# Sums of key features by ones-products for three blocks, r tiles 0 to 5 inside the M products, and loads and stores behind the transposed rows

## The chip, the cores and the metric

The kernel runs on 1 core of one Trainium2 chip. The metric is the device time of one execution in microseconds (us). The record also gives, for all runs but the first ones of the kernel before, the mean clock that was granted to TensorE, as a share of full speed. A kernel's *profile* shows one execution instruction by instruction; its length is called the *span*, and is some 1.7 us less than the device time of the same execution. No run here is recorded as slow. Kernels that were sent together ran on the same chip, and the kernel before ran in between them in the same rounds.

## The reference, cut to what matters

The result is the output of one transformer block (linear attention, then a gated MLP) and the gradients of all its inputs. Only the forward attention matters for the change:

```python
# S = 2048 rows, D = 640, 32 heads of 20
qkv = layernorm(x) @ wqkv
pq, pk = phi(q), phi(k)              # phi(t) = (t > 0 ? t + 1 : exp(t)) + 1e-6
kv  = einsum("bhsd,bhse->bhde", pk, v)
z   = einsum("bhsd->bhd", pk)        # the sums of the key features
num = einsum("bhqd,bhde->bhqe", pq, kv)
den = einsum("bhqd,bhd->bhq", pq, z)[..., None] + 1e-6
o   = num / den
h   = x + merge_heads(o) @ wo
# then h2 = h + mlp(layernorm(h)), and the gradients by jax.vjp
```

The kernel divides the features of a row by that row's `den` before they meet `kv`; the product `r = pq / den` is what is called r below. There are 16 row tiles of 128 rows, and 5 blocks of 128 feature columns.

## The kernel before

Its first 135 us go in this order: the rows are normalised and transposed, multiplied by wqkv to give key features (`pk_all`), which are in turn multiplied with the rows (the *M products*, one of five blocks at a time). Then come the small products that fold M, wqkv and wo into one matrix Wp, and then the residual and the MLP. Into these the q tiles and the r tiles are woven. Helpers and order, with cuts:

```python
def phi(acc, dst, then=None):          # a q tile: exp, relu on ScalarE, the rest on VectorE later
    ...
    A.activation(two(mq[:]), acc[:, :, 0:HD], AF.Exp)
    A.activation(two(rq[:]), acc[:, :, 0:HD], AF.Relu)
    def rest():
        V.tensor_scalar(out=mq[:], in0=mq[:], ..., op0=ALU.min, op1=ALU.add)      # L276
        V.tensor_tensor(out=dst, in0=mq[:], in1=rq[:], op=ALU.add)                # L277
    held.append(rest)

def z_late(ms, acc):                   # key sums: one-column products with ones
    for t in range(ST):
        for i, m in enumerate(ms):
            T.matmul(acc[:, i:i + 1], lhsT=pk_all[:, t, m * P:(m + 1) * P], rhs=ones[:, 0:1], ...)
    A.copy(out=Z[:, ms[0]:ms[-1] + 1], in_=acc[:, 0:len(ms)])
    for m in ms:
        z_diag(m)

def z_row(ms, acc):                    # the sums as a row on all partitions: Zb
    ...
    A.copy(out=Zb[...], in_=acc[:, 0:len(ms) * P])                                # L324

def r_prod(t):                         # pq * Zb: GpSimd for t < 6, else VectorE
    ...
    (G if t < 6 else V).tensor_tensor(out=pr[t, j], in0=pqs[t][:, js], in1=Zb[:, js], op=ALU.mult)

def r_red(t):   ... V.reduce_sum(...)                                             # L343
def r_inv(t):   ... V.tensor_scalar(... add 1e-6); V.reciprocal(...)              # L346, L347
def r_scale(t): ... V.tensor_tensor(... pqs[t] * 1/den)                           # L350
def r_T(t):     dmaT(out=pqT[:, :, t * P:(t + 1) * P], in_=pqs[t])   # transposing DMA, SyncE queue

# the K loop: trickle holds the loads of wqkv's last part, w1, w3 and wo, in this order
for t in range(ST):
    k = p1_mm(t, D)
    ...
    if i == 1 and g > 0:
        group_out(g - 1)               # stores pk (and, for the first two groups, the rows)
    elif t >= 2 and trickle:
        trickle.pop(0)()

# the M products, blocks 1 to 4 (cut)
m_end(1)
z_late((3, 4), big())                  # blocks 0 to 2 get their sums as a 321st column of M
m_part(2, range(8))
z_row((0, 1), big())
q_tile(5)
m_part(2, range(8, ST))
m_end(2)
...
m_part(3, range(5))
z_row((2, 3, 4), big())
r_prod(0)
...                                    # three r tiles are finished in this stage, five more later
```

Of the kernel before, what the change touches and what calls it, by code (L numbers as in the profile page):

```python
# [9 lines left out]
P = 128  # L10
# [45 lines left out]
def kernel(  # L56
# [119 lines left out]
    def load_wq(a, b):  # L176
        dma(out=wqkv[:, :, a * HD:b * HD], in_=wq_v[:, :, a * HD:b * HD])
# [42 lines left out]
    def load_w13(c0, c1):  # L220
        def go1():
            dma(out=w1[:, c0:c1, 0:F], in_=rows(B_w1)[:, c0:c1, :])

        def go3():
            dma(out=w3[:, c0:c1, :], in_=rows(B_w3)[:, c0:c1, 0:F - FL])
        return [go1, go3]
# [101 lines left out]
    def r_prod(t):  # L328
        for j in range(2):
            js = slice(j * HD, (j + 1) * HD)  # L330
            if t < 6:
                pr[t, j] = (p1.tile([P, HD], F32, name="pr", bufs=2) if t % 2 else
                            pf.tile([P, HD], F32, name="pr", tag="h2", bufs=2))[:]
            else:
                pr[t, j] = ps.tile([P, 512], F32, name="prp", tag="at", bufs=2)[:, 0:HD]
            (G if t < 6 else V).tensor_tensor(out=pr[t, j], in0=pqs[t][:, js], in1=Zb[:, js], op=ALU.mult)

    def heads(ap):
        return ap.rearrange("p (h e) -> p h e", e=DH)
# [40 lines left out]
    def m_part(m, tiles):  # L380
        if m not in macc:
            macc[m] = [ps.tile([P, 512], F32, name="macc", tag=("m", "tr")[m % 2], bufs=2) for _ in range(2)]
        for t in tiles:
            for j, n in enumerate((HD, HD + (m < 3))):
                T.matmul(macc[m][j][:, 0:n], lhsT=pk_all[:, t, m * P:(m + 1) * P],  # L385
                         rhs=x_ext[:, t, j * HD:j * HD + n], start=(t == 0), stop=(t == ST - 1))

    def m_end(m):
        mb = mbs[:, m % 4, :]
        acc = macc.pop(m)  # L390
        for j in range(2):
            A.copy(out=mb[:, j * HD:(j + 1) * HD], in_=acc[j][:, 0:HD])
        if m < 3:
            A.copy(out=Z[:, m:m + 1], in_=acc[1][:, HD:HD + 1])
            z_diag(m)
        if m < DT - 1:
            dmaT(out=mT[:, :, m * P:(m + 1) * P], in_=mb)
# [13 lines left out]

    def load_w2T(a, b):
        dmaT(out=w2T[:, :, a:b], in_=B_w2[a:b, :])

    trickle = []

    zero_pads()
    load_w2T(0, 2 * P)
# [19 lines left out]
            ln1.part(x_sb, t + 1, 0)  # L438
            p1_norm(t)
    ln1.part(x_sb, 3, 1)  # L440
    trickle += [lambda: load_wq(4, 6)]
    for c0, c1 in ((0, 2), (2, 4), (4, 5)):
        trickle += load_w13(c0, c1)
    trickle += [lambda: dma(out=w1[:, :, F:FP], in_=rows(B_w3)[:, :, F - FL:F])]
    trickle += [lambda: dma(out=wo[:], in_=A_wo.rearrange("(c p) n -> p c n", p=P))]



    stat_of = {t: (t + 4,) for t in range(7)}
    stat_of.update({7: (11, 12), 8: (13,), 9: (14,), 10: (15,)})  # L450
# [7 lines left out]
    def group_out(g):  # L458
        sl = slice(g * TPC, (g + 1) * TPC)
        dma(out=pk_v[:, sl, :], in_=pk_all[:, sl, :])  # L460
        if g < 2:
            xn_out(g, dma)

    QT = (5, 7, 9, 11)
    for t in range(ST):
        g, i = divmod(t, TPC)
        k = p1_mm(t, D)
        if t < 3:
            p1_tr(t + 1, ((0, 2), (2, DT)))
        for n in stat_of.get(t, ()):  # L470
            ln1.run(x_sb, n, n + 1)
            if on_act(n):
                ln1.bias(n)
        for n in norm_of.get(t, ()):
            if not on_act(n):
                p1_norm(n)
        phi_rest(t < 4)
        phi(k, pk_all[:, t, :])
        for n in norm_of.get(t, ()):
            if on_act(n):  # L480
                p1_norm(n)
        if t in QT:
            q_tile(QT.index(t))
        if 2 <= t < 6:
            ghh_chunk(t - 2, ps.tile([P, 2, 512], F32, name="gp", tag="big", bufs=2)[:, 0])
            p1_tr(t + 2)
        if t >= 3:
            m_part(0, [t - 3])
        if t >= 11:
            V.memset(bd[:, t - 11, :], 0.0)  # L490
            make_mask(t - 11)
        if t >= 9:
            m_part(1, [2 * (t - 9), 2 * (t - 9) + 1])
        if i == 1 and g > 0:
            group_out(g - 1)
        elif t >= 2 and trickle:
            trickle.pop(0)()
    phi_rest()
    group_out(SC - 1)

    def big():
        return ps.tile([P, 2, 512], F32, name="bigx", tag="big", bufs=2)[:, 0]

    q_tile(4)
    m_part(0, (13, 14, 15))
# [1 line left out]
    phi_rest()  # L507
    m_part(1, (14, 15))
    m_end(1)
    z_late((3, 4), big())  # L510
    m_part(2, range(8))
    z_row((0, 1), big())
    q_tile(5)
    m_part(2, range(8, ST))
    m_end(2)
    load_w2T(4 * P, 8 * P)
    phi_rest()
    m_part(3, range(5))
    z_row((2, 3, 4), big())
    r_prod(0)  # L520
    q_tile(6)
    m_part(3, range(5, 11))
    phi_rest()
    r_red(0)
    r_inv(0)
    r_prod(1)
    q_tile(7)
    kvT_block(0, big())
    m_part(3, range(11, ST))
    phi_rest()  # L530
    r_scale(0)
    r_T(0)
    r_red(1)
    r_inv(1)
    r_prod(2)
    m_end(3)
    load_g2T(1)
    dmaG(out=m_v[:, 0:4, :], in_=mbs[:])
    m_part(4, range(5))
    q_tile(8)  # L540
    kvT_block(1, big())
    m_part(4, range(5, 11))
    phi_rest()
    r_scale(1)
    r_T(1)
    r_red(2)
    r_inv(2)
    r_prod(3)
    q_tile(9)
    m_part(4, range(11, ST))  # L550
    m_end(4)
    r_prod(4)
    phi_rest()
    r_scale(2)
    r_T(2)
    ps.release()
    load_x(0, 2)
    while trickle:
        trickle.pop(0)()


    ps = pool("pap", space=PSUM)
# [74 lines left out]
    def r4_out():  # L637
        dmaG(out=r_v[:, 0:4, :], in_=pq6[:, 0:4, :])

    def r4b_out():  # L640
        dmaG(out=r_v[:, 4, :], in_=pqs.pop(4))

    def r_load(t):
        pqs[t] = pf.tile([P, D], BF16, name="pql", bufs=4)[:]
# [131 lines left out]
    def run(*steps):  # L776
# [4 lines left out]
    pkx.append(p1.tile([P, DT + 6, D], BF16, name="pkx", tag="pk"))  # L781
    run((q_late, 10, f2_mT), (f2_kv, 2), (f2_kv, 3), (f2_kv, 4), (phi_rest,), (q_late, 11), (f2_wT, 0), (f2_wT, 1),
        (phi_rest,), (q_late, 12), (f2_wT, 2), (f2_wT, 3), (phi_rest,), (q_late, 13, lambda: f2_wT(4)),
        (r_red, 3), (r_inv, 3), (r_scale, 3), (r_prod, 5), (load_x, 2, 4), (r_T, 3), (q_late, 14), (r_red, 4),
        (r_inv, 4), (r_scale, 4), (r_T, 4), (load_x, 4, 8), (mlp_ghh, 4), (q_late, 15),
        (sig_table,), (f2_half, 0, 0), (f2_half, 1, 0), (f2_half, 0, 1), (f2_half, 1, 1), (f2_hn, 0), (mlp_ghh, 5),
        (f2_half, 2, 0), (f2_hn, 1), (f2_m_out,), (load_w2T, 8 * P, 10 * P), (f2_half, 2, 1),
        (f2_ht, 0), (mlp_ghh, 6), (f2_half, 3, 0), (f2_hn, 2), (f2_w_out,), (f2_ht, 1), (f2_half, 3, 1), (phi_rest, 2),
        (q_out, 10, 14), (f2_ht, 2), (f2_hn, 3), (mlp_ghh, 7), (f2_half, 4, 0), (f2_ht, 3),
        (f2_half, 4, 1), (r4_out,), (r_red, 5), (r_inv, 5), (r_scale, 5), (r_out, 5), (r4b_out,), (q_out, 8, 10))  # L790
    p1.release()
    pa = pool("pa", "right")

# [25 lines left out]
    def r_end(t):  # L819
        r_scale(t)  # L820
        r_out(t)

    r_steps = [{1: ((r_den, 6),), 2: ((r_end, 6), (r_load, 8)), 4: ((r_den, 7), (r_load, 9)), 5: ((r_end, 7),),
                6: ((xn_out, 2, dmaG),), 3: ((load_w2T, 10 * P, F),), 12: ((r_load, 10),), 13: ((xn_out, 3, dmaG),)},
               {0: ((r_den, 8),), 1: ((r_end, 8), (r_load, 11)), 2: ((r_den, 9),), 3: ((r_end, 9), (r_load, 12)),
                4: ((r_den, 10), (q_rest,)), 5: ((r_end, 10), (r_load, 13)), 6: ((r_den, 11),),
                7: ((r_end, 11), (r_load, 14)), 9: ((r_den, 12),), 10: ((r_end, 12), (r_load, 15))},
# [596 lines left out]
```

## Time and profile before

| | value |
|---|---|
| median of 3 timed runs | 839.07 us (838.42 to 840.68) |
| span of the profiled execution | 832.4 us (its device time was 834.09) |
| TensorE busy / idle in it | 819.1 / 13.3 us |
| its granted clock | 1.0 |

TensorE is busy nearly always, so the kernel can only be made faster by removing work from TensorE, by filling its idle stretches (*holes*), or by raising its clock. The prediction prints the lines. Note the difference of some 5 us in device time between the timed runs and the profiled one: it turns out to matter.

### The profile page before, as it was taken

To read this page: it belongs to the slowest core of one execution; us is meant where nothing else is said; L and a number is where in the kernel's file an instruction comes from. 1 tells how busy PE (TensorE), PEld (TensorE's weight loads), DVE (VectorE), ACT (ScalarE), POOL (GpSimd) and SP (SyncE) were. 2 spreads that over 40 slices of the span, in tenths; PEclk is the share of its full clock that TensorE was granted. 3 is DMA by queue.
4 is the path that set the end of the run, shared out by engine and by line. 5 is a ranking of instruction groups with operands and counts; after the bars stand their busy time and mean duration, and the time that the engine had idled before them with its cause. 6 is when DMAs were issued, how large, how long until landed. Compare 5 with 4: busy or idle time off the path is not lost.

```text
span 832.4 us, 14209 instructions
## 1 busy us (share of the span) xinstructions
PE 819.1 (98%) x5552; PEld 523.8 (63%) x5552; DVE 454.1 (55%) x964; ACT 319.5 (38%) x606; POOL 106.6 (13%) x156
## 2 busy tenths in 40 slices
PE   8899998999999999999999999999999999999998
PEld 6577644555555555777777777777777777555554
DVE  7847898999898656400047777772681445200000
ACT  6765777755555666111122221222211433211111
POOL 3214232122122010000001111110220000000000
PEclk9999999999999999999999999999999999999999
DMA  9986899786574465999968888346997688885771
GB/s 270 324 236 136 221 236 290 223 226 149 166 203 118 127 215 171 202 253 244 264 149 181 181 205 204 86 102 113 227 267 148 153 189 184 208 194 140 163 169 37
DMA packets 323315, 157.59 MB, mean 189 GB/s; under 512 B 235312, under 2 KB 318160, under 8 KB 323248
## 3 DMA queue, kind: packets, MB, share of 16 engines
q1 hardware_dynamic: 293696, 127.73, 64.0%
q10 hardware_dynamic: 24416, 11.23, 6.5%
q0 software_dynamic: 5136, 17.73, 6.1%
q8 instruction: 43, 0.70, 0.3%
q14 instruction: 24, 0.20, 0.1%
HBM read 48.15 MB, written 51.46 MB: 120 GB/s over the span
## 4 chain that ended last, share of the span: by engine, by line
PE 92%; DVE 3%; DMA 3%; ACT 1%; SPq 1%; issue 0%; DVEq 0%; ACTq 0%
PE job L1189 19%; PE mm L364 18%; PE ghn L991 14%; PE gxn L1348 8%; PE o L751 7%; PE gw L944 7%; PE big L255 3%; PE gwo L1076 3%; PE dkv L1292 3%; PE gr L1048 3%; PE macc L385 2%; PE at L573 2%; DMA pqT<-x_sb 1%; PE mm L255 1%; DMA g2T<-in_grad_out_dram 1%; DMA pqT<-pql 1%
## 5 line engine op out<-in xcount | busy, mean ns | idle before, releaser
L1189 PE MATMUL job<-gb,hnN 128*128 128x432 bf16 x640 | 117.0, 346 | 0.0
L991 PEld LDWEIGHTS <-ggb 128*128 128x128 bf16 x864 | 84.5, 98 | 32.8
L1189 PEld LDWEIGHTS <-hnN 128*128 128x128 bf16 x640 | 62.6, 98 | 54.1
L364 PE MATMUL mm<-pqT,w 128*128 128x512 bf16 x405 | 93.8, 379 | 1.3 <-ACT gate L693 1.2
L364 PEld LDWEIGHTS <-w 128*128 128x128 bf16 x540 | 52.8, 98 | 64.7 <-issue 1.8
L1193 ACT CAST obs<-job 128x432 bf16<-128x432 f32 (+1 forms) x60 | 29.2, 486 | 123.1 <-PE job L1189 120.7
L751 PE MATMUL o<-w,hhT 128*128 128x320 bf16 x448 | 67.5, 299 | 0.0
L364 PE MATMUL mm<-g2T,w2T 128*128 128x512 bf16 x260 | 64.6, 379 | 0.2 <-ACT gate L693 0.2
L991 PE MATMUL ghn<-w13a,ggb 128*128 128x320 bf16 x448 | 63.5, 299 | 0.0
L991 PE MATMUL ghn<-w13b,ggb 128*128 128x320 bf16 x416 | 61.4, 299 | 0.0
L751 PEld LDWEIGHTS <-hhT 128*128 128x128 bf16 x448 | 43.8, 98 | 23.6
L944 PE MATMUL gw<-g,hb 128*128 128x320 bf16 x416 | 57.0, 299 | 0.0
L374 ACT CAST ghh<-mm 128x512 bf16<-128x512 f32 x52 | 30.6, 589 | 53.7 <-PE mm L364 52.9
L944 PEld LDWEIGHTS <-hb 128*128 128x128 bf16 x416 | 40.6, 98 | 15.7
L1348 PE MATMUL gxn<-wqT,gT 128*128 128x320 bf16 x320 | 48.7, 299 | 0.0
L1056 POOL TENSOR_TENSOR sz<-Zb,g_h 128x640 f32<-128x640 bf16 x16 | 20.2, 1261 | 199.4 <-DVE g_h L1054 199.4
L691 ACT ACTIVATE sig<-mm 128x512 bf16<-128x512 f32 x56 | 33.6, 601 | 27.6 <-PE mm L364 24.6
L364 PEld LDWEIGHTS <-w2T 128*128 128x128 bf16 x280 | 27.2, 98 | 26.6 <-issue 1.7
L255 PE MATMUL big<-wqkv,pqT 128*128 128x320 bf16 x260 | 39.3, 299 | 4.0 <-DMA pqT<-x_sb 3.2
L1003 ACT ACTIVATE gs<-ghn 128x640 bf16<-128x640 f32 x16 | 11.3, 704 | 78.6 <-PE ghn L991 78.6
L255 PEld LDWEIGHTS <-pqT 128*128 128x128 bf16 x320 | 30.4, 98 | 17.0 <-DMA pqT<-x_sb 3.5
L1348 PEld LDWEIGHTS <-gT 128*128 128x128 bf16 x320 | 31.3, 98 | 12.2
(196 smaller groups left out, 1249.9 us busy)
## 6 DMA issues: line engine op xcount, KB each, us to landing
hh_d<-hhT SPq DMA_DIRECT2D x24, 256.0 KB, 2.8
gg_d<-gate SPq DMA_DIRECT2D x24, 256.0 KB, 3.1
gg_d<-ghh POOLq DMA_DIRECT2D x24, 256.0 KB, 3.3
ggb<-gg_d SPq DMA_DIRECT2D x6, 896.0 KB, 5.7
ggb<-gg_d SPq DMA_DIRECT2D x6, 832.0 KB, 7.0
out_dram<-obs ACTq DMA_DIRECT2D x40, 108.0 KB, 2.3
x_sb<-in_A_x_dram SPq DMA_DIRECT2D x6, 640.0 KB, 5.9
ggb<-gg_d SPq DMA_DIRECT2D x2, 1728.0 KB, 12.9
```

The lines of the kernel that those rows point to most:

```text
L255: T.matmul(acc, lhsT=pqT[:, c, t * P:(t + 1) * P], rhs=wqkv[:, c, n0:n0 + HD], start=(c == 0), stop=(c == DT - 1))
L364: T.matmul(acc[:], lhsT=w[:, c, fc * P:(fc + 1) * P], rhs=rhs[:, c, :], start=(c == 0), stop=(c == DT - 1))
L374: A.copy(out=ghh[n // 2][:, n % 2, :], in_=acc[:])
L691: A.activation(sig[:, i, :], gp[:], AF.Sigmoid)
L751: T.matmul(o2["ps"][:, 0:HD], lhsT=hhT[c][:, fc, i * P:(i + 1) * P], rhs=w2[:, fc, j * HD:(j + 1) * HD], start=(fc == 0), stop=(fc == FT - 1))
L944: T.matmul(acc[:, j, 0:HD], lhsT=hb[b][:, t, i * P:(i + 1) * P], rhs=g2[:, t, j * HD:(j + 1) * HD], start=(t == 0), stop=(t == ST - 1))
L991: T.matmul(acc[:, j, 0:HD], lhsT=ggb[t // 2][:, k, lo:lo + P], rhs=rhs[:, j * HD:(j + 1) * HD], start=(k == 0), stop=(k == NG - 1))
L1048: T.matmul(gr[t][:, j, 0:HD], lhsT=ghT[t][:, c, :], rhs=wT2[:, c, j * HD:(j + 1) * HD], start=(c == 0), stop=(c == DT - 1))
L1076: T.matmul(acc[m][:, j, 0:n], lhsT=r_sb[:, t, m * P:(m + 1) * P], rhs=g_hx[:, t, j * HD:j * HD + n], start=(t == 0), stop=(t == ST - 1))
L1189: T.matmul(acc[:, 0:n], lhsT=lhs[:, t, m * P:(m + 1) * P], rhs=rhs(t), start=(t == 0), stop=(t == ST - 1))
L1193: A.copy(out=ob, in_=acc[:, 0:n])
L1348: T.matmul(acc[:, j, 0:HD], lhsT=g, rhs=wqT[:, k, j * HD:(j + 1) * HD], start=(k == 0), stop=(k == 14))
```

## The change

Its intent is to fill the holes of the first 135 us. The last load of wqkv no longer stands ahead of the row transposes, and the stores meet them later; the key sums are complete one M block earlier, so that the r tiles can start earlier; six r tiles instead of three are then done inside the M products, and fewer are left for the crowded start of the MLP. The diff, cut to its core:

```diff
-            if t < 6:                                   # r_prod: which tiles GpSimd multiplies
+            if t < 8:
-            for j, n in enumerate((HD, HD + (m < 3))):  # block 2 loses its 321st column
+            for j, n in enumerate((HD, HD + (m < 2))):
-    trickle += [lambda: load_wq(4, 6)]
-    ... w1, w3, wo in the same list
+    trickle = {3: w13[0], 4: w13[1], 11: lambda: load_wq(4, 6), 12: w13[2], 14: w13[3], 15: load_wo}
+    outs = {6: ((group_out, 0),), 7: ((xn_out, 0, dma),), 10: ((group_out, 1), (xn_out, 1, dma)), 13: ((group_out, 2),)}
@@ the M products @@
     m_end(1)
+    for go in w13[4:]:
+        go()
-    z_late((3, 4), big())
+    z_late((2, 3, 4), big())
     m_part(2, range(8))
     z_row((0, 1), big())
+    z_row((2, 3, 4), big())
+    r_prod(0)
     q_tile(5)
+    r_prod(1)
     m_part(2, range(8, ST))
     m_end(2)
+    r_head(0)                   # r_red, r_inv, r_scale, r_T
     load_w2T(4 * P, 8 * P)
+    r_prod(2)
     ... so on, one r tile a q tile: r_head(1) to r_head(5), r_prod(3) to r_prod(7)
@@ the MLP's start @@
-        (r_red, 3), (r_inv, 3), (r_scale, 3), (r_prod, 5), (load_x, 2, 4), (r_T, 3), (q_late, 14), (r_red, 4),
-        (r_inv, 4), (r_scale, 4), (r_T, 4), (load_x, 4, 8), (mlp_ghh, 4), (q_late, 15),
+        (r_red, 6), (r_inv, 6), (r_scale, 6), (load_x, 2, 4), (r_T, 6), (q_late, 14), (load_x, 4, 8), (load_g2T, 1), (r_store, 4, 6),
+        (mlp_ghh, 4), (q_late, 15),
... (tiles 6 and 7 were done with DVE inside the MLP; stores and two transposing loads change places)
```

More of the change, by code (lines that the diff above doesn't have):

```diff
@@ L335, in r_prod @@
                 pr[t, j] = ps.tile([P, 512], F32, name="prp", tag="at", bufs=2)[:, 0:HD]
-            (G if t < 6 else V).tensor_tensor(out=pr[t, j], in0=pqs[t][:, js], in1=Zb[:, js], op=ALU.mult)
+            (G if t < 8 else V).tensor_tensor(out=pr[t, j], in0=pqs[t][:, js], in1=Zb[:, js], op=ALU.mult)
     def heads(ap):
@@ L392, in m_end @@
             A.copy(out=mb[:, j * HD:(j + 1) * HD], in_=acc[j][:, 0:HD])
-        if m < 3:
+        if m < 2:
             A.copy(out=Z[:, m:m + 1], in_=acc[1][:, HD:HD + 1])
@@ L413, in load_w2T @@
         dmaT(out=w2T[:, :, a:b], in_=B_w2[a:b, :])
-    trickle = []
     zero_pads()
@@ L440, with load_wo @@
     ln1.part(x_sb, 3, 1)
-    trickle += [lambda: load_wq(4, 6)]
-    for c0, c1 in ((0, 2), (2, 4), (4, 5)):
-        trickle += load_w13(c0, c1)
-    trickle += [lambda: dma(out=w1[:, :, F:FP], in_=rows(B_w3)[:, :, F - FL:F])]
-    trickle += [lambda: dma(out=wo[:], in_=A_wo.rearrange("(c p) n -> p c n", p=P))]
+    w13 = [go for c0, c1 in ((0, 2), (2, 4), (4, 5)) for go in load_w13(c0, c1)]
+    w13 += [lambda: dma(out=w1[:, :, F:FP], in_=rows(B_w3)[:, :, F - FL:F])]
+    def load_wo():
+        dma(out=wo[:], in_=A_wo.rearrange("(c p) n -> p c n", p=P))
+    trickle = {3: w13[0], 4: w13[1], 11: lambda: load_wq(4, 6), 12: w13[2], 14: w13[3], 15: load_wo}
     stat_of = {t: (t + 4,) for t in range(7)}
@@ L460, in group_out @@
         dma(out=pk_v[:, sl, :], in_=pk_all[:, sl, :])
-        if g < 2:
-            xn_out(g, dma)
+    outs = {6: ((group_out, 0),), 7: ((xn_out, 0, dma),), 10: ((group_out, 1), (xn_out, 1, dma)), 13: ((group_out, 2),)}
     QT = (5, 7, 9, 11)
     for t in range(ST):
-        g, i = divmod(t, TPC)
         k = p1_mm(t, D)
@@ L493 @@
             m_part(1, [2 * (t - 9), 2 * (t - 9) + 1])
-        if i == 1 and g > 0:
-            group_out(g - 1)
-        elif t >= 2 and trickle:
-            trickle.pop(0)()
+        for f, *n in outs.get(t, ()):
+            f(*n)
+        if t in trickle:
+            trickle[t]()
     phi_rest()
@@ L502, in big, with r_head @@
         return ps.tile([P, 2, 512], F32, name="bigx", tag="big", bufs=2)[:, 0]
+    def r_head(t):
+        r_red(t)
+        r_inv(t)
+        r_scale(t)
+        r_T(t)
     q_tile(4)
@@ L509 @@
     m_end(1)
-    z_late((3, 4), big())
+    for go in w13[4:]:
+        go()
+    z_late((2, 3, 4), big())
     m_part(2, range(8))
     z_row((0, 1), big())
+    z_row((2, 3, 4), big())
+    r_prod(0)
     q_tile(5)
+    r_prod(1)
     m_part(2, range(8, ST))
     m_end(2)
+    r_head(0)
     load_w2T(4 * P, 8 * P)
+    r_prod(2)
     phi_rest()
     m_part(3, range(5))
-    z_row((2, 3, 4), big())
-    r_prod(0)
     q_tile(6)
+    r_head(1)
+    r_prod(3)
+    phi_rest()
     m_part(3, range(5, 11))
-    phi_rest()
-    r_red(0)
-    r_inv(0)
-    r_prod(1)
     q_tile(7)
     kvT_block(0, big())
+    r_head(2)
+    r_prod(4)
+    phi_rest()
     m_part(3, range(11, ST))
-    phi_rest()
-    r_scale(0)
-    r_T(0)
-    r_red(1)
-    r_inv(1)
-    r_prod(2)
     m_end(3)
-    load_g2T(1)
     dmaG(out=m_v[:, 0:4, :], in_=mbs[:])
+    r_head(3)
+    r_prod(5)
     m_part(4, range(5))
@@ L541 @@
     kvT_block(1, big())
+    r_head(4)
+    r_prod(6)
+    phi_rest()
     m_part(4, range(5, 11))
+    q_tile(9)
+    r_head(5)
+    r_prod(7)
     phi_rest()
-    r_scale(1)
-    r_T(1)
-    r_red(2)
-    r_inv(2)
-    r_prod(3)
-    q_tile(9)
     m_part(4, range(11, ST))
     m_end(4)
-    r_prod(4)
-    phi_rest()
-    r_scale(2)
-    r_T(2)
     ps.release()
     load_x(0, 2)
-    while trickle:
-        trickle.pop(0)()
     ps = pool("pap", space=PSUM)
@@ L638, in r4_out, with r_store @@
         dmaG(out=r_v[:, 0:4, :], in_=pq6[:, 0:4, :])
-    def r4b_out():
-        dmaG(out=r_v[:, 4, :], in_=pqs.pop(4))
+    def r_store(a, b):
+        for t in range(a, b):
+            dmaG(out=r_v[:, t, :], in_=pqs.pop(t))
     def r_load(t):
@@ L788 @@
         (f2_ht, 0), (mlp_ghh, 6), (f2_half, 3, 0), (f2_hn, 2), (f2_w_out,), (f2_ht, 1), (f2_half, 3, 1), (phi_rest, 2),
-        (q_out, 10, 14), (f2_ht, 2), (f2_hn, 3), (mlp_ghh, 7), (f2_half, 4, 0), (f2_ht, 3),
-        (f2_half, 4, 1), (r4_out,), (r_red, 5), (r_inv, 5), (r_scale, 5), (r_out, 5), (r4b_out,), (q_out, 8, 10))
+        (q_out, 10, 14), (f2_ht, 2), (f2_hn, 3), (mlp_ghh, 7), (load_w2T, 10 * P, F), (f2_half, 4, 0), (f2_ht, 3),
+        (f2_half, 4, 1), (r4_out,), (r_red, 7), (r_inv, 7), (r_scale, 7), (r_T, 7), (r_store, 6, 8), (q_out, 8, 10))
     p1.release()
@@ L821, in r_end @@
         r_out(t)
-    r_steps = [{1: ((r_den, 6),), 2: ((r_end, 6), (r_load, 8)), 4: ((r_den, 7), (r_load, 9)), 5: ((r_end, 7),),
-                6: ((xn_out, 2, dmaG),), 3: ((load_w2T, 10 * P, F),), 12: ((r_load, 10),), 13: ((xn_out, 3, dmaG),)},
+    r_steps = [{2: ((r_load, 8),), 4: ((r_load, 9),), 6: ((xn_out, 2, dmaG),), 12: ((r_load, 10),),
+                13: ((xn_out, 3, dmaG),)},
                {0: ((r_den, 8),), 1: ((r_end, 8), (r_load, 11)), 2: ((r_den, 9),), 3: ((r_end, 9), (r_load, 12)),
```

## The prediction

> **What bounds the kernel now.** I read the page's first part, then a table of busy time by stretches, then who TensorE waited for, then the timelines around those waits.
>
> ```profile
> PE 819.1 (98%) x5552; PEld 523.8 (63%) x5552; DVE 454.1 (55%) x964; ACT 319.5 (38%) x606; POOL 106.6 (13%) x156
> ```
>
> TensorE (PE) is busy 819.1 of 832.4 us. All its idle time is 13.3 us, so whatever the change does elsewhere, it gains only what it takes from these 13.3 us. The stretches (columns: us, PE, PEld, DVE, ACT, POOL busy with instruction counts, clock, DMA share, GB/s) say where they lie:
>
> ```profile
> core 0: us, PE busy (x) PEld busy (x) DVE busy (x) ACT busy (x) POOL busy (x), PEclk, DMA share, GB/s
> 0.00:56.00 56.00, 50.11 (x378) 35.49 (x379) 42.19 (x133) 38.00 (x63) 15.75 (x38) 1.00 1.02 294
> 56.00:78.00 22.00, 22.00 (x197) 16.16 (x196) 13.02 (x32) 10.72 (x26) 8.70 (x11) 1.00 0.52 124
> 78.00:92.00 14.00, 14.00 (x131) 10.53 (x129) 11.73 (x29) 13.04 (x34) 1.54 (x2) 1.00 0.88 160
> 92.00:103.00 11.00, 10.50 (x78) 6.42 (x76) 9.59 (x28) 6.45 (x13) 4.59 (x7) 1.00 0.95 254
> 103.00:134.00 31.00, 27.93 (x143) 13.62 (x141) 28.65 (x60) 21.43 (x43) 9.63 (x14) 1.00 0.96 259
> ...
> 350.00:832.40 482.40, 478.60 (x3443) 324.81 (x3441) 179.13 (x359) 105.80 (x195) 31.33 (x35) 1.00 0.78 177
> ```
>
> 5.9 us are lost before 56 (K projections), nothing at 56 to 92 (M products and the small products after them), 0.5 at 92 to 103, 3.1 at 103 to 134 (start of the MLP), where VectorE (DVE) is 92% busy. The last 3.8 us, nearly all the end of the program, the change does not touch. The waits of PE by releaser (total, times, longest) name three:
>
> ```profile
> PE big L255 <- DMA pqT<-x_sb: 3.2, 1, 3.2
> PE at L573 <- DMA pqT<-pql: 1.7, 1, 1.7
> PE mm L364 <- ACT gate L693: 1.4, 2, 1.2
> ```
>
> In PE's timeline they are single holes. By the starts of the instructions on both sides they are a little longer than the brackets say (0.15 us each): 3.36, 1.35 and 1.81, and a small one of 0.38 at 117.6.
>
> ```profile
> 35.31 2.89 PE L255 MATMUL big<-wqkv,pqT 128*128 128x320 bf16 x20 [3.19 <-DMA pqT<-x_sb]
> ...
> 125.99 1.24 PE L364 MATMUL mm<-pqT,w 128*128 128x512 bf16 x5 [1.20 <-ACT gate L693]
> ...
> 132.26 0.85 PE L573 MATMUL at<-Wp,pqT 128*128 128x320 bf16 x5 [1.66 <-DMA pqT<-pql]
> ```
>
> The first hole comes from the SyncE queue:
>
> ```profile
> 24.01 1.21 SPq L242 DMA_TRANSPOSE pqT<-x_sb  x1
> 25.26 0.57 SPq L460 DMA_DIRECT2D pk_d<-pk_all  x1
> 25.88 0.61 SPq L456 DMA_DIRECT2D xn_d<-x_sb  x1
> 26.59 3.03 SPq L242 DMA_TRANSPOSE pqT<-x_sb  x1
> 29.67 0.60 SPq L222 DMA_DIRECT2D w<-in_B_w_dram  x1
> 31.02 1.23 SPq L242 DMA_TRANSPOSE pqT<-x_sb  x1
> ```
>
> The transpose of row tile 9 is issued at 26.59 behind two 640 KB stores, and behind loads of wqkv, w1 and w3 (800, 864 and 832 KB) issued from 14.3 on. It lands 8.7 us later, at 35.3; PE was done with everything else at 31.95. The last of these eight transposes, with little ahead, lands in 3.8 us. The other two holes come from DVE at the MLP's start: the chain of waits runs from 106 to 126 mostly through DVE, then through one transposed r tile (issued 126.33, landing 5.88 us later).
>
> [...] the min/add step (L276) takes 0.32 us as a rule, but 0.94 at 66.6, beside GpSimd products, and the add after it 0.89 instead of 0.49.[...] Here 32 one-column products take 0.78 us, 24.4 ns each.[...]
>
> **The change, part by part.**
>
> *Sums for block 2 by ones-products.* 16 more one-column products at 24.4 ns: +0.39 us on PE, before the second M product ends. One column less in 16 products of 321 (a start every 136 ns for 320, so 0.43 ns a column) is under 0.01 us. What it buys: the whole of Zb is there before that product instead of after it, so GpSimd's first product starts near 60.7 instead of 65.05. A side cost: the three small products now take the two "big" PSUM buffers in turn, so q tile 5 waits for the copy of the first Zb part (0.37 us on ScalarE), which used to be hidden. Estimate +0.3 us.
>
> *Transposes ahead of loads.* The wqkv load (800 KB) leaves the place ahead of row 8, and both stores leave the place ahead of row 9. At 375 GB/s, as seen around 20 us, the wqkv load is 2.2 us of queue. Row 9 should land near 30.4 (26.6 + 3.8), before PE wants it at 31.95. The next limits: row 10 is normalised by ScalarE at 31.0 anyway, one store ahead, landing about 35.4, wanted at 35.5. Row 11 is issued near 33 behind the second store, landing 37 to 38, wanted at 37.7. Also ScalarE is late with PSUM buffers there, worth 0.15. I take 0.45 us of 3.36 as left: gain 2.9 us. The loads now come after 38 us; w1 and w3 are wanted at 102.7, wo at 81.8, the moved wqkv at 68.7, so none of these should be seen.
>
> *r of tiles 0 to 5 inside the M products.* One tile on DVE, reduce, +1e-6, reciprocal, scale, without GpSimd beside it, is 91.13 - 88.89 = 2.24 us:
>
> ```profile
> 88.89 0.87 DVE L343 TENSOR_REDUCE rden<-pr 128x16 f32<-128x320 f32 x2
> 89.79 0.18 DVE L346 TENSOR_SCALAR rden<-rden 128x32 f32<-128x32 f32 x1
> 90.00 0.35 DVE L347 RECIPROCAL rden<-rden 128x32 f32<-128x32 f32 x1
> 90.39 0.82 DVE L350 TENSOR_TENSOR pql<-pql,rden 128x640 bf16<-128x640 bf16 x1
> 91.13 0.48 DVE L578 TENSOR_TENSOR x_sb<-at,x_sb 128x320 bf16<-128x320 f32 x1
> ```
>
> With GpSimd beside it, it is some 2.5 us (step L346 takes 0.48). Before q tile 10, DVE now does six such tiles instead of three: +7.5 us. From the first product's end (62.2) to 80.0, where the masks of the last three kv blocks are due, DVE was idle for 4.8 us before. So the masks come some 2.5 us late. PE can take 0.8 us (blocks masked by 81.0, their first reader starts at 81.8) plus the 0.7 us by which PE itself is later. I put down a new hole of 1.0 us before the first wo product. In the stretch after it DVE has one r tile to do instead of two, and catches up by the first residual add.
>
> *Less at the MLP's start.* Tiles 6 and 7 cost DVE there 2.2 us (product, reduce, reciprocal; 109.08 to 111.28) and 0.73 (scale) each: 5.9 us of the 28.65 go away. The rest, 22.8 of 31, leaves air: a pair of chunks then asks DVE for about 6 us, while its 30 products of 0.216 us and the next row tile hold PE for over 7. So the holes 0.38 and 1.35 should close. The r tile that PE waited for at 130.6 is now transposed from about 107 on: 1.81 closes. Sum 3.54; I take 3.4.
>
> *Moved without effect.* The second grad_out transpose and the last w2 transpose change places near 93 to 105; their readers come after 110. From 134 on, nothing of the order of PE's work changes.
>
> Sum: -2.9 + 0.4 + 0.3 + 1.0 - 3.4 = -4.6 us. The measured median is 839.07 (without the profiler, some 5 us more than in the profiled run); the difference should carry over: 834.5 us.
>
> **The rivals.** (A) *VectorE becomes the bound in the M products.* There PE has no hole now, and what DVE does there is doubled[...]. For it: DVE would be busy for nearly all of 62 to 83, each GpSimd product can stretch a DVE step up to threefold[...]. Against it: exp and relu buffers are three deep, one q tile comes each 3 to 4 us, and the kv blocks ask for their masks only at 80. If the lateness is 5 us instead of 2.5, the hole is 3.5 us: about 837. (B) *The row transposes wait all the same*, now for the norms: DVE is 89% busy from 20 to 40, even with PE standing still for 3 us of it. If PE comes earlier it meets DVE's lag in rows 10 to 13. Against it: row 9 itself is normalised at 26.4, and later rows by ScalarE in turn. At worst half of the gain goes: about 836. (C) *The MLP's start waits for transfers, not for DVE.* ScalarE waited 3.9 us there for stores of gg to free their buffers, and DMA engines are busy all the time (0.96); the transposes moved forward fall into a stretch at 0.95. Against it: DVE's records have hardly a gap there, and the stores are issued late because their data are late. This would keep some 2 us: 836.5. (D) *All goes well*: no hole in the M products, rows in time: -6 us, 833.
>
> **Range and chances.** A and B or A and C together give 838.5; D with a lucky run, 831.5. So 831.5 to 838.5, centre 834.5. Faster by over 2% would be under 822.3, a gain of 16.8 us, and all PE idle time is 13.3 us: practically excluded, 0.01. Slower by over 2% needs 17 us of new holes, which no wait above comes near: 0.005. Within 2%: 0.985.
>
> **What would show it.** In the changed profile: the wait of PE for the transposed x rows falls from 3.2 to under 0.6 in total, and those transposes land in about 4 us. The stretch 103 to 134 (shifted by 1 to 2 us) shows PE above 30.5 of 31 and DVE near 23. No PE wait for a transposed r tile. In the stretch 56 to 78, DVE rises from 13 to 19 or 20 and GpSimd from 8.7 to about 12. Then the two costs: a wait of q tile 5 for the Zb copy (0.3 us), and one of the wo products for the masks or of the kv blocks' buffers (about 1 us). The last part, 482 us from 350 on, keeps its length within 0.3 us. I am wrong if the new holes between 56 and 92 add up to over 2.5 us, if the x-row wait stays above 1.5, or if the MLP's start keeps over 1 us of holes; then the step named in A, B or C failed. A change outside the first 140 us would refute the whole picture.

## The result, and the profile after

| | before | after |
|---|---|---|
| median, first comparison | 839.21 (838.42 to 840.68, 4 runs) | 832.00 (831.65 to 833.04, 4 runs) |
| ratio, first comparison | | 0.9914 [0.9897, 0.9931] |
| ratio, later comparison (e6) | | 0.9946 [0.9927, 0.9966] |
| ratio, later comparison (e11) | | 0.9942 [0.9928, 0.9957] |
| span of the profiled execution | 832.4 | 830.0 |

A ratio is the mean time of one kernel's fast runs over that of the other's fast runs of the same rounds, with its 95% interval; so it is not quite the ratio of the medians. The change is a small real gain, within 2%: 0.9% in the first comparison, 0.5 to 0.6% in the two later ones. The profiled spans, both at clock 1.0, differ by only 2.4 us.

First the totals of the changed kernel, from the page's first part, to be held against the first fence of the prediction:

```profile
PE 818.9 (99%) x5540; PEld 523.8 (63%) x5568; DVE 454.3 (55%) x960; ACT 319.4 (38%) x605; POOL 110.2 (13%) x160
```

TensorE's work is the same, 818.9 us; idle fell from 13.3 to 11.1. Next the busy time by stretches of the changed kernel, with the columns of the prediction's table, cut at the same events as before (all of it lies 2 us earlier):

```profile
0.00:54.00 54.00, 50.63 (x390) 35.83 (x393) 41.93 (x133) 38.20 (x65) 15.86 (x38) 1.00 0.88 247
54.00:76.00 22.00, 21.71 (x201) 15.93 (x198) 17.23 (x39) 9.73 (x23) 11.80 (x15) 1.00 1.08 271
76.00:90.00 14.00, 12.67 (x116) 9.30 (x116) 11.95 (x30) 11.65 (x32) 3.11 (x5) 1.00 0.77 137
90.00:101.00 11.00, 10.58 (x77) 6.63 (x76) 8.53 (x25) 7.44 (x15) 3.56 (x6) 1.00 0.98 246
101.00:132.00 31.00, 30.23 (x158) 15.25 (x159) 26.25 (x52) 23.51 (x47) 9.49 (x14) 1.00 1.04 284
348.00:830.00 482.00, 478.19 (x3439) 324.02 (x3437) 179.23 (x359) 105.72 (x195) 31.34 (x35) 1.00 0.78 177
```

Idle TensorE time in the five early stretches went 5.9, 0, 0, 0.5, 3.1 before; it is now 3.4, 0.3, 1.3, 0.4, 0.8. The holes did move: the first and the fifth stretch have 2.5 and 2.3 us less of them (what is left in the first lies at the program's start), the second and third have new ones. The last 482 us are unchanged. The waits of TensorE by releaser (total, times, longest) of the changed kernel say what the new ones are:

```profile
PE wt L610 <- DVE bd L205: 0.7, 1, 0.7
PE kv L404 <- DMA mT<-mbs: 0.6, 1, 0.6
...
PE mm L364 <- ACT gate L693: 0.5, 1, 0.5
...
PE big L255 <- ACT Zb L324: 0.3, 1, 0.3
```

The waits for transposed x rows and for a transposed r tile are gone. New are a wait of the wo products for DVE's masks (`bd`, 0.7), of the kv products for the fourth transposed M block (0.6) and of q tile 5 for the copy of Zb (0.3). The SyncE queue of the changed kernel, around the former hole, carries row transposes with a store between them; the wqkv load is gone from ahead of them (it is issued at 45.2), while the first loads of w1 and w3 still stand there, issued at 14.8 and 16.4:

```profile
24.44 3.62 SPq L242 DMA_TRANSPOSE pqT<-x_sb  x2
28.11 0.57 SPq L458 DMA_DIRECT2D pk_d<-pk_all  x1
31.72 1.21 SPq L242 DMA_TRANSPOSE pqT<-x_sb  x1
```

The transposes of rows 8 to 11 landed in 3.7, 2.6, 2.6 and 4.1 us, where row 9 had needed 8.7.

To see where the time went, I measured three intervals on TensorE's timeline in every profiled execution: to the start of the key-sum products; from there to the first MLP product; and from there to the last group of gradient products (640 of them, which take 116.8 us). The three add up to the span but for its last 120.3 us, which are as long in both.

| profiled execution | to the sums | sums to MLP | MLP to last group |
|---|---|---|---|
| before | 56.06 | 46.60 | 609.42 |
| after | 53.67 | 49.32 | 606.70 |
| after minus before | -2.39 | +2.72 | -2.72 |

The three differences add to -2.4 us, exactly that of the spans. So at the same clock the loads and stores bring all of the gain, and what the r tiles take from the MLP's start they give back in the M products.

### The profile page after: what moved, and what is told of

The parts are those of the page before. It is cut to its first block, busy times and chain, and to the rows that moved or that the text cites. A ratio compares the mean times of both kernels' runs of the same rounds, so it can differ in the third digit from the quotient of the medians.

```text
span 830.0 us, 14209 instructions
## 1 busy us (share of the span) xinstructions
PE 818.9 (99%) x5540; PEld 523.8 (63%) x5568; DVE 454.3 (55%) x960; ACT 319.4 (38%) x605; POOL 110.2 (13%) x160
## 4 chain that ended last, share of the span: by engine, by line
PE 88%; ACT 1%; DMA 1%; issue 0%; DVE 0%; ACTq 0%
PE mm L364 20%; PE job L1189 19%; PE ghn L991 14%; PE gxn L1348 8%; PE o L751 7%; PE gw L944 7%; PE gwo L1076 3%; PE dkv L1292 3%; PE gr L1048 3%; PE at L572 2%; PE mm L255 1%; PE dkv L1221 1%; DMA gg_d<-gate 1%; PE gt L923 0%; PE wt L610 0%
## 5 line engine op out<-in xcount | busy, mean ns | idle before, releaser
L364 PE MATMUL mm<-g2T,w2T 128*128 128x512 bf16 x245 | 62.9, 379 | 1.1 <-ACT gate L693 0.5
L374 ACT CAST ghh<-mm 128x512 bf16<-128x512 f32 x52 | 30.5, 587 | 55.0 <-PE mm L364 50.1
L255 PEld LDWEIGHTS <-pqT 128*128 128x128 bf16 x320 | 30.5, 98 | 14.3 <-ACT pqT L251 2.2
## 6 DMA issues: line engine op xcount, KB each, us to landing
ggb<-gg_d SPq DMA_DIRECT2D x6, 832.0 KB, 7.2
```

Of the source, the lines that this page charges most:

```text
L255: T.matmul(acc, lhsT=pqT[:, c, t * P:(t + 1) * P], rhs=wqkv[:, c, n0:n0 + HD], start=(c == 0), stop=(c == DT - 1))
L364: T.matmul(acc[:], lhsT=w[:, c, fc * P:(fc + 1) * P], rhs=rhs[:, c, :], start=(c == 0), stop=(c == DT - 1))
L374: A.copy(out=ghh[n // 2][:, n % 2, :], in_=acc[:])
```

## The experiments

Twelve runs were made, in three groups of four (e1 to e4, e5 to e8, e9 to e12); each holds several executions. All gave correct results, and no run was in the slow state.

**Separating the parts: e1 to e4.** Theory: the gain is one of the loads' order, plus a gain of the r tiles that their cost eats. Rival: the timed runs of the kernel before had larger holes than its profiled one, so the holes are worth more than the profile shows. First the kernel before once more, unchanged, to see its spread:

> The kernel before, unchanged, to see which of its executions the first profile was. Its timed runs were 838.4 to 840.7 us, its profiled execution 834.1 us (span 832.4), while the changed kernel's profile (span 830.0) is as its timed runs. Theory X: the holes of TensorE before 140 us vary between executions of the kernel before, and the first profile was a lucky one: then a new profile has a span of 836 to 839 us and larger holes at the transposed rows of x or at the start of the MLP, the rest being equal. Theory Y: the profiled execution of any kernel is shorter on that chip: then the new profile is again near 832 and the timed runs near 839.

Measured: 835.51 (834.04 to 836.55, 4 runs), ratio 0.998 [0.9957, 1.0003]. Its profile has the same holes as the first one (3.4 us at the x rows, 1.5 at the gate, 1.4 at the r tile). But the four times sort by granted clock: 834.04 and 834.76 at 1.0, 836.26 and 836.55 at 0.998. So the spread goes with the clock. That the holes were no larger at 0.998 isn't shown for this kernel: its two kept profiles are both at 1.0, and a span of 833.0 us fits neither theory as it stood.

Then the order of loads and stores alone, in the kernel before:

```diff
-    trickle += [lambda: load_wq(4, 6)] ...            # one list, popped from t = 2 on
+    trickle = {3: w13[0], 4: w13[1], 11: lambda: load_wq(4, 6), 12: w13[2], 14: w13[3], 15: load_wo}
+    outs = {6: ((group_out, 0),), 7: ((xn_out, 0, dma),), 10: (...), 13: ((group_out, 2),)}
     m_end(1)
+    for go in w13[4:]:
+        go()
     z_late((3, 4), big())
```

> The kernel before with only the order of loads and first stores changed (w1, w3, wo, wqkv loads and pk, xn stores behind the transposed rows); sums and r as before. My theory: the hole at the transposed x rows (3.2 us in the first profile, perhaps more in the timed runs) goes, the holes at the start of the MLP stay at about 3 us: 834 to 836.5 us if the rows' hole is the larger share of the 7.2 us gained, ratio 0.994 to 0.997. Rival: the rows' hole is worth little, and r is what counts: ratio above 0.997.

Measured: 831.44 (831.06 to 834.06, 6 runs), ratio 0.9936 [0.9917, 0.9956]: the whole gain of the change, and more than the 834 to 836.5 us that I had expected. One of the six, 834.06, was at clock 0.997. Its intervals are 53.15, 46.60, 609.31: the first gains 2.9, the other two are those of the kernel before. The holes at the MLP's start stay, as they should.

Then the rest of the change, with the old order of loads and stores:

```diff
-    trickle = {3: w13[0], 4: w13[1], 11: ..., 15: load_wo}
-    outs = {...}
+    trickle += [lambda: load_wq(4, 6)] ...            # as before
```

> The changed kernel with the loads and first stores back in their old order; sums by ones-products, r of tiles 0 to 5 inside the M products, and the moved transposes as in the change. My theory: the 3.2 us hole at the x rows is back, the MLP start is without holes, the new holes between 56 and 92 are as in the changed kernel (about 1.6 us): 835 to 837.5 us, ratio 0.995 to 0.998. If the two parts add up, the gains of this and of the run with the loads alone give the 7.2 us; if they overlap, the sum is well over it.

Measured: 836.45 (834.89 to 838.53, 6 runs), ratio 0.9993 [0.997, 1.0015]: nothing, where I had expected 0.995 to 0.998. Its intervals are 59.40, 49.36, 606.27: the r tiles cost 2.76 us before the MLP and save 3.15 after it. (The first number holds an x-row hole of 3.3 us, one of 0.9 more, and a stretch at clock 0.50 behind them, of the kind that e4 shows next.)

Last the ones-products alone:

```diff
-            for j, n in enumerate((HD, HD + (m < 3))):
+            for j, n in enumerate((HD, HD + (m < 2))):
-    z_late((3, 4), big())
+    z_late((2, 3, 4), big())
     z_row((0, 1), big())
+    z_row((2, 3, 4), big())
     ...
-    z_row((2, 3, 4), big())
```

> The kernel before with only the sums of block 2 by ones-products and both parts of Zb before q tile 5; r_prod and r stay where they were. It measures the cost of this piece alone: 0.39 us for 16 products and 0.3 us of waiting for the copy of the first part of Zb, visible in the profile at about 56 to 60 us; in the time 0 to +1 us, within noise.

Measured: 837.78 (837.24 to 839.79, 4 runs), ratio 1.0013 [0.999, 1.0036]. Between the sums and the kv products TensorE took 24.24 us instead of 23.42, so +0.8; 0.3 of it is the wait for the Zb copy. The time does not resolve it.

This profile showed something more. The same x-row hole as before was followed by half clock. TensorE's busy time and clock by stretches of 2 us (e4), and the group after the hole in its timeline:

```profile
36.00:38.00 2.00, 2.00 (x13) 0.83 1.07 363
38.00:40.00 2.00, 2.00 (x9) 0.50 1.07 397
40.00:42.00 2.00, 2.00 (x13) 0.82 1.17 323
42.00:44.00 2.00, 2.00 (x17) 1.00 1.11 359
```

```profile
35.98 4.25 PE L255 MATMUL big<-wqkv,pqT 128*128 128x320 bf16 x20 [3.09 <-DMA pqT<-x_sb]
```

The columns of the first are us, PE busy (count), clock, DMA share and GB/s. The engine counts as fully busy all the time, but 20 products take 4.05 us by their starts where they took 2.72, and the two following stretches are slow as well: 1.7 us are lost, after a hole that itself cost some 3.1. So this hole was charged twice, and busy time does not show it. Half clock for 3.4 us (which loses 1.7) is half of 3.4/832, or 0.2% of the mean clock: by this estimate, a run at mean clock 0.998 had one such episode.

The half clock did not follow every such hole. By the starts of the instructions on both sides the hole was 3.26 us in this profile (32.72 to 35.98) and 3.47 in e3's, and clock 0.50 followed both; it was 3.36 in the first profile of the kernel before and 3.52 in that of e1, and the clock stayed at 1.0. So two profiles with this hole show it and two do not, and what decides is not in the traces. That it is a matter of chance, and with it the time of the kernel before, is my guess; it was not shown.

**Testing the clock: e5 to e7.** If the half clock comes from the hole, the kernel before gets faster when TensorE is given useless work in the hole. First with a little:

```diff
         g, i = divmod(t, TPC)
+        if t == 9:
+            keep = ps.tile([P, 512], F32, name="keep", tag="tr", bufs=2)
+            for _ in range(32):
+                T.matmul(keep[:, 0:P], lhsT=ones[:], rhs=ones[:], start=True, stop=True, ...)
         k = p1_mm(t, D)
```

> The kernel before with 32 dummy products of ones (128 x 128) on TensorE just ahead of the products of row tile 9, where it waits for the transposed row anyway. They do nothing for the result. Theory: part of what the change gains is not the hole itself but what follows it: in the runs with the sums alone and with r alone the profile shows a granted clock of 0.50 for about 3.5 us from 2 us after the hole begins to close, costing some 1.7 us, and the kernel before shows a mean clock of 0.996 to 0.998 in 10 of 11 runs. If so, this kernel with the hole unfilled but TensorE kept busy has clock 1.0 in nearly all runs, and a median near the best runs of before: 834 to 835 us, ratio 0.996 to 0.998. Rival: the clock drop is from something else (total load, chip) and stays: then the ratio is 1.000 or above and the clocks remain at 0.998.

Measured: 838.19 (836.64 to 841.24, 6 runs), ratio 1.0021 [0.9996, 1.0046]: not faster. The clocks were 1.0 in four runs of six, 0.999 and 0.997 in the others, and yet the times are long. Its profile has an x-row hole of 1.6 us as intended, but also waits later on that the kernel before doesn't have: 2.1 us for a transposed block in the backward part (`dkv` for `xnT`, landing 13.5 us where it took 6.9 at most), 0.9 for Wp (as in e8 below) and 0.5 for a small load. What made these, chance or the 64 extra instructions, I could not settle. This run shows the clock kept in four of six executions (in two of eleven of the kernel before beside it); by its time it confirms nothing, and taken alone it speaks against the theory.

The changed kernel again, and the loads alone again, in the same rounds:

> The changed kernel, unchanged, beside the next run on the same chip: about 831.5 to 832.5 us, clock 1.0 in all runs, ratio 0.991 to 0.994.

> The kernel with the loads and first stores alone, on the same chip as the changed kernel. Theory: moving r gains 2.5 us at the MLP's start (holes of 1.5 and 1.2 us in the first look) and loses as much to the new holes and the added products (0.39 sums, 0.3 Zb copy, 0.6 kv products waiting for the fourth M transpose, 0.7 masks, plus 0.15 each): so it equals the changed kernel within 1 us: 831 to 832.5. Rival, my prediction's own sum for r: the changed kernel is 1.7 us faster than this one.

Measured: 831.84 for the changed kernel (ratio 0.9946 [0.9927, 0.9966], a little above the expected 0.991 to 0.994) and 831.86 (830.83 to 832.59, 6 runs; 0.9943 [0.9924, 0.9962]) for the loads alone. They are equal, and the rival, 1.7 us for the r part, is out. Yet their profiles are not: the waits of TensorE in e7 still hold both MLP holes of the kernel before,

```profile
PE mm L364 <- ACT gate L694: 1.4, 1, 1.4
PE at L574 <- DMA pqT<-pql: 1.4, 1, 1.4
```

while the intervals of e6 are 53.13, 49.35, 606.77 against 53.05, 46.60, 609.14 of e7. The r part moves 2.6 us of waiting from after the MLP's first product to before it, and no more.

**Can the r part be made to pay? e8 and e10.** Three small waits in the M stage have named releasers. Each was given another way: another PSUM buffer for Zb, the fourth M transpose ahead of the r transposes in the SyncE queue, one r tile later so that DVE is free for the masks.

```diff
-    z_row((2, 3, 4), big())
+    z_row((2, 3, 4), ps.tile([P, 512], F32, name="bigy", tag="tr", bufs=2)[:])
-    load_w2T(4 * P, 8 * P)              # after r_head(0)
-    r_head(2)
+    r_red(2); r_inv(2); r_scale(2)
     m_end(3)
+    r_T(2)
+    load_w2T(4 * P, 8 * P)
     q_tile(9)
-    r_head(5)
-    r_prod(7)                           # both to the list after q tile 13
```

> The changed kernel with its three new holes treated: the second part of Zb uses another PSUM buffer (so q tile 5 does not wait for the Zb copy), the fourth M transpose is issued ahead of r tile 2 and of the large w2 transpose, and the r work of tile 5 (with the product of tile 7) moves behind the last wo product. Theory: the holes are separate and on the path, so 0.3, 0.6 to 0.75 and 0.7 to 0.8 us come back: 829.8 to 830.8 us, about 1.5 us less than the changed kernel on this chip. Rival: closing one lets the next wait (masks, a late r tile, the residual adds) take its place, and the gain is under 0.5 us.

Measured: 831.32 (829.87 to 832.93, 6 runs), ratio 0.9939 [0.9919, 0.996]. The three waits are gone from its profile: sums to kv 23.79 us (25.02 in the changed kernel, 23.42 in the kernel before, which has 16 products fewer there) and kv to wo products 2.31 (3.14), as in the kernel before. In their place came a wait of 0.9 us for the last transposed part of Wp, which landed in 4.0 us instead of 2.6. From the sums to the MLP it took 48.05 instead of 49.32. The time is 0.5 us under that of the changed kernel in the same rounds (e6), where I had expected 1.5; the runs don't resolve it.

Two of its six runs were at clock 0.998, and its profiled run is one of them. There the half clock followed a much shorter hole, near the start, as TensorE's timeline and its stretch from 16 to 18 us (columns as in e4) show:

```profile
15.49 2.08 PE L364 MATMUL gp<-g2T,w2T 128*128 128x512 bf16 x5 [1.80 <-DMA g2T<-in_grad_out_dram]
```

```profile
16.00:18.00 2.00, 2.00 (x10) 0.50 0.91 300
```

TensorE was busy only 1.7 of every 2 us in the 6 us ahead of this hole, with many short transposes. In e11 a hole of 1.83 us at the same product had no such effect. So the length of one hole does not decide alone; I know no more of it from these runs.

In e10 one chunk of the grad_out products was also moved ahead, against the wait at the gate:

```diff
-        (sig_table,), (f2_half, 0, 0), (f2_half, 1, 0), (f2_half, 0, 1), (f2_half, 1, 1), (f2_hn, 0), (mlp_ghh, 5),
+        (sig_table,), (f2_half, 0, 0), (f2_half, 1, 0), (mlp_ghh, 5), (f2_half, 0, 1), (f2_half, 1, 1), (f2_hn, 0),
```

> The changed kernel with its three holes treated as in the earlier run, and one independent product group moved ahead of the second halves of the first residual blocks, so that a late last Wp transpose (0.9 us of waiting in that run) is covered. Theory: z to MLP start about 47 us instead of 49.3; 829 to 830.5 us, at least 1 us under the changed kernel in the same rounds, and faster than both kernels. Rival: what is won there is lost in other waits; no difference to the changed kernel.

Measured: 830.87 (829.43 to 833.73, 6 runs), ratio 0.993 [0.9913, 0.9947]. In the same rounds the changed kernel had 832.07 (e11 below). By the means it is 1.0 us faster, but the intervals overlap: not resolved. From the sums to the MLP it took 47.66 us, where I had expected 47. The longest run of the six is the profiled one, and it shows the clock at another place. TensorE's timeline of e10:

```profile
118.73 1.24 PE L364 MATMUL mm<-g2T,w2T 128*128 128x512 bf16 x5 [3.31 <-ACT gate L694]
119.81 4.01 PE L364 MATMUL mm<-pqT,w 128*128 128x512 bf16 x10
```

A hole of 3.3 us in the MLP, and then ten products in 4.01 us, where this group takes 2.32 in the changed kernel; the clock from 120 to 122 is 0.50. It is the same charge as in e4, in another stage. ScalarE's gate came late with a store of `gate` to DRAM: on the chain that ended last, this store was issued at 111.66, landed in 6.4 us and is followed by the products at 118.73; in the changed kernel's profile it landed in 4.5 and held ScalarE's next gate for 1.91. Why it took longer in this execution stays open; the other five runs of e10 were at clock 1.0.

**A full test of the clock: e9, with e11 as the measure.** e5 had left a hole of 1.6 us and unexplained waits. Here fewer and longer products fill nearly the whole hole:

```diff
+        if t == 9:
+            keep = ps.tile([P, 512], F32, name="keep", tag="tr", bufs=2)
+            for _ in range(13):
+                T.matmul(keep[:], lhsT=ones[:], rhs=wqkv[:, 0, D:D + 512], start=True, stop=True, ...)
         k = p1_mm(t, D)
```

> The kernel before with 13 dummy products of 512 columns (2.8 us) in the hole ahead of row tile 9. The first such try (32 of 128 columns, 64 instructions more) kept the clock at 1.0 in four of six runs, yet its spans were 834.8 to 839.5 us, with later waits for transposes of Wp and xnT in its one profile that the kernel before did not show. This one adds 26 instructions and fills nearly all of the hole. Theory: the clock drop costs the kernel before about 1.7 to 2 us where it happens, and the rest of the first try's time was other transfers: clock 1.0 in at least five of six runs and a median of 833.5 to 835 us, ratio 0.996 to 0.999. Rival: the drop does not set the time (or the lost time comes back elsewhere): ratio 1.000 to 1.003 as in the first try, with the clock at 1.0.

> The changed kernel, unchanged, in the same rounds as the run with the holes treated: 831 to 832.5 us, clock 1.0.

Measured: e9 835.41 (834.8 to 836.27, 5 runs), ratio 0.9982 [0.9967, 0.9998], all five at clock 1.0; the kernel before had clock 1.0 in 1 of 11 runs of the same rounds. e11 832.07 (831.03 to 833.22; 0.9942 [0.9928, 0.9957]), all at clock 1.0. The timeline of e9 shows the useless products in the hole:

```profile
34.08 2.97 PE L470 MATMUL keep<-wqkv,ones 128*128 128x512 bf16 x13
37.57 2.89 PE L255 MATMUL big<-wqkv,pqT 128*128 128x320 bf16 x20 [0.52 <-DMA pqT<-x_sb]
```

The kernel still waits for the row (37.57 is no earlier than before), nothing useful has been done, and yet the kernel is 1.5 us faster by the ratio (0.2 to 2.8 by its interval). This profile, of the slowest of the five runs, also holds waits of 1.0 us for row 8 and of 1.0 for wqkv. So e9 puts the clock's share of the hole at some 1.5 us, in line with the 1.7 of e4's profile. In the 33 runs of the kernel before that ran beside these three groups, the means sort the same way, though the times overlap:

| mean clock of the run | runs | times | mean |
|---|---|---|---|
| 1.0 | 4 | 834.2 to 836.1 | 834.9 |
| 0.998 | 21 | 834.7 to 839.3 | 836.8 |
| 0.996 and 0.997 | 8 | 836.8 to 839.6 | 837.9 |

The changed kernel was at 1.0 in all of its 16 recorded runs.

**Loads or stores? e12.** The change moved both from ahead of row 9. Here the stores go back, and the loads stay moved:

```diff
-    outs = {6: ((group_out, 0),), 7: ((xn_out, 0, dma),), 10: ((group_out, 1), (xn_out, 1, dma)), 13: ((group_out, 2),)}
+    outs = {5: ((group_out, 0), (xn_out, 0, dma)), 9: ((group_out, 1), (xn_out, 1, dma)), 13: ((group_out, 2),)}
```

> The changed kernel with the pk and xn stores of the first and second group back at their old places, ahead of row 9; the loads stay moved. It tells which of the two moved things made the hole at row 9. My prediction's arithmetic: the two stores (1.28 MB at 375 GB/s) are 3.4 us of queue, so row 9 lands near 33.8 instead of 30.4 (wanted at 32): a hole of 1.5 to 2 us,[...] and 833 to 834 us. Rival: the loads were the greater part, and the hole stays under 0.5 us: 831.5 to 832.5.

Measured: 832.1 (831.95 to 833.89, 5 runs), ratio 0.9948 [0.9933, 0.9962], as the changed kernel. Row 9 landed in 5.9 us with the stores ahead of it, against 2.6 after and 8.7 before, but TensorE hardly waited for it (timeline of e12):

```profile
32.46 2.89 PE L255 MATMUL big<-wqkv,pqT 128*128 128x320 bf16 x20 [0.25 <-DMA pqT<-x_sb]
```

With the wqkv load of 800 KB gone from the queue, the hole is nearly closed, so moving this load is enough, and moving the stores as well is worth nothing that these runs resolve. The converse, the stores moved and the load left, was not run. By the three landings the stores take some 3.3 us and the load 2.8; a landing of 5.9 left almost no hole, so moving the stores alone might have been enough too. My expectation of a hole of 1.5 to 2 us missed: part of a transpose's landing time lies beside TensorE's other work anyway.

## Why the prediction was right, and where not

The direction was right, and so was the picture of the first 135 us. The forecast of 834.5 us lies 2.5 above the 832.0 measured, near the lower end of the range. Two of its terms and one thing left out were wrong; that their sum still comes near the gain of the later comparisons is luck.

**The loads and stores: right, for the reason given.** Gain 2.9 predicted; the first interval lost 2.9 and 3.0 us in e2 and e7, and 2.4 in the changed kernel's own profile, whose start happened to hold a wait of 1.3 us for ScalarE's mq (the exponentials of a q tile). Of the reason, e12 shows that moving the load is enough; whether the stores alone would have been is not shown.

**The M products: right in kind, too small.** The prediction put down 0.4 + 0.3 + 1.0 = 1.7 us of cost. All five profiles with this part and without the repairs (after, e3, e6, e11, e12) took 49.32 to 49.36 us from the sums to the MLP instead of 46.60: 2.7 us. How it splits between the waits for mT and for the masks changes from one to the next; the total does not, so one chain sets it. The chain is DVE's: in each of the five, the first wo product waits for the masks of the last three kv blocks (0.7 to 1.5 us) and starts 28.2 us after the sums (25.7 before), which is 2.4 of the 2.7 us. In the changed kernel the masks begin 22.4 us after DVE's first reduce, and DVE is busy 20.7 of these. The masks in DVE's timeline, before and after:

```profile
80.02 0.91 DVE L205 TENSOR_TENSOR bd<-kv,mask 128x160 bf16<-128x160 f32 x3 [0.25 <-PE kv L404]
```

```profile
81.46 0.74 DVE L205 TENSOR_TENSOR bd<-kv,mask 128x160 bf16<-128x160 f32 x3
```

Before, DVE waited for the kv products there; after, it does not. Counted from the sums the masks begin 3.8 us later (27.8 against 24.0), where I had put "some 2.5"; in the stretch 54 to 76 its busy time is 17.2 us, where I had put 19 or 20. One r tile of the changed kernel on DVE, with the next q tile's step after it:

```profile
67.82 0.87 DVE L343 TENSOR_REDUCE rden<-pr 128x16 f32<-128x320 f32 x2
68.72 0.48 DVE L346 TENSOR_SCALAR rden<-rden 128x32 f32<-128x32 f32 x1
69.23 0.35 DVE L347 RECIPROCAL rden<-rden 128x32 f32<-128x32 f32 x1
69.62 0.97 DVE L350 TENSOR_TENSOR pq<-pq,rden 128x640 bf16<-128x640 bf16 x1
70.51 0.48 DVE L276 TENSOR_SCALAR mq<-mq 128x640 bf16<-128x640 bf16 x1
```

From reduce to the end of scale this is 2.7 us (67.82 to 70.51), beside GpSimd's products, where I had used "some 2.5" by stretching only L346 (0.48 us instead of 0.18). The scale is stretched as well: it takes 0.97 in all six tiles, each beside a product for some 0.3 us or more, and 0.82 in the kernel before where no product runs beside it. Six tiles of 0.2 us are 1.2: that is the size of what is missing, though I have not shown each piece of it. That DVE sets this stage is rival A in part. The r transposes also stand in the SyncE queue ahead of the fourth M transpose, which was not foreseen; the wait of the kv products for it (0.6) costs nothing of its own, for in e3 and e12 it is absent and the wo products start no earlier.

In e8, with one r tile fewer ahead of them, the masks begin 19.3 us after the first reduce instead of 22.4; both waits are gone and, net of the new wait for Wp, 1.3 of the 2.7 us with them.

**The MLP's start: right in kind, too large.** Gain 3.4 predicted. The third interval is 606.63 us on average in the five profiles with the r part and 609.35 in the five without it and without other changes there (before, e1, e2, e7, e9; e4 had 609.96, and e5 612.73 with its later waits): 2.7. The r-tile hole and the larger one at the gate closed. The small hole, some 8 us ahead of the latter, did not: it holds 0.2 to 0.8 us in three of the five, a wait of 1.1 for another transpose stands in its place in e12, and where it is absent (e11) the gain is 3.4. There ScalarE waited 1.9 us in the changed kernel (0.8 before) for the store of `gate` to free its buffer, so this is rival C in part. DVE was busy 26.25 of 31 us, not "near 23", and TensorE 30.23, not 30.5; probably more of the MLP now falls into that stretch.

**So the r part and the sums together bring about 0 instead of -1.7 us.** The step that failed is the term "+1.0" for the masks, with the cost of one r tile beside GpSimd under it: the sums and the Zb copy cost 0.8 (e4; predicted 0.7), which leaves 1.9 for the masks. Three slips in the sums change little: 7.5 less 4.8 is 2.7, not 2.5; rivals A and C together give 839.0, not 838.5; and the one-column products start every 25.0 ns (31 steps in 0.776 us), not 24.4.

**The clock: not priced.** The prediction took the difference of some 5 us between timed and profiled runs for the profiler's and let it carry over to the changed kernel. That was wrong: the first profiled execution of the kernel before kept clock 1.0 through its hole of 3.36 us, while 29 of 33 later runs had a mean clock below 1.0 (where they lost it is not in the record; e3 and e4, with the same hole, lost it there). A run of the kernel before at 0.998 takes 1.9 us more than one at 1.0 (836.8 against 834.9), the changed kernel has no such hole, and so the loads' order is worth some 2.9 + 1.9 us rather than 2.9. At clock 1.0 the two kernels stand at 834.9 (4 runs) and 832.1 (16 runs).

The sum as measured: -2.9 (holes) - 1.9 (clock) + 2.7 - 2.7 = -4.8 us, against -4.6 predicted, and against 4.2 to 5.1 us in the later comparisons. The two errors, 1.7 and 1.9 us, offset each other by chance.

**What stays open.** The first comparison gave 7.2 us, some 2 more. There the kernel before ran at 838.4 to 840.7, longer than most of its 33 later runs (834.2 to 839.6), and the clocks of those first runs are not recorded. More lost clock would explain it; it isn't shown.

## What to carry to other kernels

Look at a hole of TensorE of some 3 us twice: here it cost its length, and in three of five profiles some 1.7 us of clock behind it, which showed only in the granted clock and in the durations of products after it, not in busy time; so close such a hole before smaller ones, and compare timed runs with their clocks beside them. Work that is moved out of a crowded stage is not free in the stage that had no hole: here it filled the slack of VectorE (20.7 of 22.4 us busy up to the masks), and a sum of durations that took only one step of an r tile as longer beside GpSimd's products (L346, 0.48 us instead of 0.18), and not the scale (0.97 instead of 0.82), came out too small. When two parts of a change are each forecast to be worth a few us, run each alone: here one part had all of the gain.
